# Turned tiles by transposing transfers of 1 MB for two tiles instead of 512 KB for one, with other buffer rings and a new order of the work

## The chip, the core and the metric

The kernel runs on one core of one Trainium2 chip. The metric is the time of one execution in device microseconds (us); lower is better. Data lie in HBM, in on-chip memory of 128 partitions, and in PSUM, the accumulators that the matrix engine writes. The engines have separate instruction queues and wait for one another by semaphores: PE (matrix multiply), DVE (vector), ACT (scalar functions), POOL (a second elementwise engine) and SP (which here only issues transfers).

## What is computed

An attention through 49 agent rows per batch, then a feed-forward layer with a softmax gate (SoLU) and a normalisation over the 1024 hidden values. There are 4 batches of 12608 tokens with 128 channels. Cut to what matters:

```python
def _attn_ref(q, k, v, agents):
    ...
    a2k = sm(agents, k)          # 49 x 12608 per batch
    agent_v = a2k @ v            # 49 x 128
    q2a = sm(q, agents)          # 12608 x 49
    return q2a @ agent_v

def _moe_ref(x, w_in, w_out, g_ln):
    h = x @ w_in                                  # 50432 x 1024
    e = np.exp(h - h.max(-1, keepdims=True))
    sm = e / (e.sum(-1, keepdims=True) + 1e-09)
    solu = h * sm
    mu = solu.mean(-1, keepdims=True)
    var = ((solu - mu) ** 2).mean(-1, keepdims=True)
    ln = (solu - mu) / np.sqrt(var + 1e-06) * g_ln
    return ln @ w_out                             # 50432 x 128
```

## The kernel before

Tokens are handled in 394 tiles of 128. A batch first runs **phase A** (L600 to L753): its keys and values come in 13 chunks, scores, exponentials and the sums over tokens give a small matrix, which is multiplied with w_in. The first batch's phase A opens the program; those of the other three run between the tiles of the batch before. **Phase B** (L862 to L909) makes, for eight tiles at a time, the softmax of the queries against the agents, as the stationary operand `pT`.

Each tile x then goes through this chain, and its names are those of the profile:

- **H** (L954, PE): four 128x512 products into `ph`, one of two PSUM buffers of 1024 columns.
- **max** (L985, DVE): copies `ph` to `e` and takes the row maximum; **exp** (L992, ACT) writes over `ph`; **U** (L1000, DVE) multiplies the two into `u`, one of six buffers. The next H on this `ph` waits for U.
- **square** (L1020, ACT): the sum of squares of `u`.
- **turning**: the second product needs `u` with the 1024 hidden values on the partitions. 63 of the 394 tiles (two in 13, and the last two) are turned on PE (L1026) and copied out of PSUM by ACT or DVE (L1031) into a `t` buffer. The other 331 are split into two 16-bit halves, F0 (L1008 on POOL, or L1006 on ACT) and F1 (L1011, POOL), in an `f` buffer, and SP issues a transposing transfer from `f` to an `x` buffer (L1015).
- **W** (L1047, PE): 24 16-bit products of 128x128 for such a tile (8 of 32 bits for one turned on PE), added up in a PSUM bank `px` that holds four tiles.
- **output**: DVE (L1100) or ACT (L1098) scales four tiles into `ob`, and SP stores eight tiles at a time (L1106).

There are five `f` buffers of 512 KB, eight `x` and eight `t` buffers of 512 KB. The `x` and `t` buffers also take the first batch's keys and values (L583, L589). SP issues everything that moves, in one order: transposing transfers, keys (L583), values (L589), queries (L841) and stores (L1106). An instruction that waits on SP holds all that stands behind it.

The order of all engines is a table. `plan.op` (L175) declares each piece of work with its engine, its cost and what it depends on; `Plan.run` (L188) walks the compressed list `STEPS` and emits the pieces in that order, and a bit beside each entry picks the engine where two are allowed. The costs decide only how many filler products PE runs in waits at the start (L1116), and which PSUM bank a piece takes. For a transposing transfer the four numbers in L1195 are what the planner assumes of it: how long SP is held (`XHOLD`), the shortest distance between two landings, the time from the hold's end to the landing (`XLAG`), and its kind.

```python
F1[x] = op("G", F(c_f1, x), 2.098, at(x, DF1, DUR, DUL), [F0[x]])
XT[x] = op("S", F(c_x, x), (XHOLD, 1.95, XLAG, 1), at(x, DX, DUR, DUL),
           [F1[x], W[fl[-1 - XB]] if len(fl) > XB else mdone[0][0]],
           after=[XT[fl[-2]] if len(fl) > 1 else None])
```

Of the kernel before, what the change touches and what calls it, by code (L numbers as in the profile page):

```python
# [13 lines left out]
F32 = mybir.dt.float32  # L14
# [3 lines left out]
F16 = mybir.dt.float16  # L18
# [11 lines left out]
    "VtHE%Qy5VvJ%YylIydemA0P_$CR8toyFdhy*0z&Jm*HgWZ9zPg(0=Itu^ZoT@{io;7N9r@!EC6}2?EYX|&FGz!sWSVQzTOMq{{3$imTjre6!Krc_zS;G"  # L30
    "YCWz30GOqY$N808r>Qy5%NLYj_Ew;)sIP3U;U?ajoAKTOsC&_$I+<B0U!*}DJbC%)YY*OE#hY+zHn|=qP8|((b1?TDFSH#?uA&XqRdoLYdjDy2@5mP9b"
    "wXW5*byc(DMJ7oLr2513)=f{E`9PdfBuuoaI3O0+__y=5d7L#DwH6=qmD=Ywx3f~w=3(s=Zq?}d>%fajxDABI=CvDZ&%LMLDAN}J+wg{f<K*vWq_NDb8"
    "bR|*>WMkdhoHQ3@*}PV8n$BlCx{`L7lG$b)@Cq#B5QQ$LCRIn$<c`dxzBLL|JG&bdGNUKKo)Ns{n4@EmD5zckDD5b{f;+2|PH+bWOu<P`MA){V@CB6b<"
    "m0R1_bEs%QGiaBq45;7`=g6BWSz(hIw^$o?z8=0^YgtG~QcK!YUtPk*5i+B~?DsR?dsc&Yfm_KTyPB`z`}AGSZDZ40N+I*YfKphcPrwn)wEgml4hD-60"
    "J4Lv>-O#HEt02EOB^m9Vi0a`{}wRKAuIezczqeZv{F9*DpH25Ty7P)Ic_MEK1D^Lge@!dB2nyYC2bANpMrLqoWeHVJ4b@uVCF7-A7>Fr8`&BH*E{i#|#"
    "qd=7kO3``|JbP6%hznP<T`<yu55K&<4MC7=YFwl+J7*2D;KSdB!jYC2pf=GI7)on~z;g0*Q7i7DduWwFB~jf!^^Ji1ypWKb(&x~gaR!il9pK;pARN#ve"
    "60C*{}Yd%PJ2l09_c3CJ?GcYuQxu;2tDd3Ssh!KJ?o8R>?ssJ1HM>rd8bPrwmMQat1HTB_FBa{UVWsZk?&2;6p=jlp0e!(P*#-Mu_jm`uoK)Fd)l`QDX"
    "#vE46=Hd+y+B!F69gVGyP=`QHhJ%$6T4;`F7USy8oQod%;IqR5&<EmhOw`-Vd}8b<E}Mn9ANeDn5hSLDKRZ>bZ~HbP$x*?r9&!Rwjh#^|fiTPSi@3<Tv"
    "gvA7P}CUeZz+fSKx#{s3&}FE3R;^tQNQ-Yw4;4uj%_#%C@F&sQ|m?cReF>V#=8Tz6hL_n#l6+$tE!fQkVSrg1`NCUq6bGCtGxB<Lqoz5n6ITjV<v;3{*"
    "-^EEvUo$U{NjkI=1fliD)`jk4uV84|*1*=NFGk@L%4giuu9WDL!ffir2+S(CLFT5EjlnI%kc4!<q=qvCXc(PP{Fm<Bk9KQSszNyJtVe*BEhR{TX!hgWC"  # L40
    "N55?AJ%j73)p+X_>8NuN4+adZ<(A9`x`=1EHSgYZb3V;IMVt3@H;uuo+GPx<z9;ZwKhxc+EVQH9r_(C}q5F_uG732}*-v1r9csc3NP)?R4dl_D+BnyYP"
    "vw?6T##`HGT6tx^jx;@Dhlm<H1L3svX6dKh9CXg_n&<H&oaFG*?;rToqVOMRrqVAdY_h%;f-+clM(w!huz%-qi4`Ejt@M#QR-5r)S9U={~~1n(YF<sf2"
    "izE;>XcdFLy~ZzU?}`Q$*AXxX~D>y0_AG@9Dx$?%@6H(n-Jju&w(ps4edC!K3oh9Ui)AaGJWD`zjv_oo<zQe>Fl#fn#_&_c-U2+Mjp#$cO~{^;`LvK%V"
    "pKB7T={x|XSTRNhpinq34I1T1*05LF`n>1N`q00@raS2Bw61n>}M2qBK+4-T3Z2H-wC9NVWaOGlKoJ{d;9yLh&^6r!L0?@k^_RkQoWDbGo!YoFRP@$C>"
    "Pho6rWW(_al6g7&!1OHTZy6iAg^s!H`6$5Mo$=tg+K|D1LxITcFWB5dE)sfFn)GF`Lfrsq5-(RFlDoJ(w*INAUjmgEzIgu4<Fpl|sS}`@;4#!HH-|ebR"
    "JArfPy_iTLq$1cULqI;wp*tO9Xy+zf&I#<_-stWrc$ISuuv@+Df{T1wx-wflQ+=o$m(nApt!u6UmQLx~oghwdkeLrNAx|Eh-J(nQy?*=@it=*0iePt(A"
# [24 lines left out]
    "t7~MeQgxp;!s3&ffAhtrfB4gnMn3i-dm&_r84Bu3eV*Wfr}^*ywdXK7;XO}k_D=0eZ^yGrve9z)xQPrNKXP+Ncdw8UC+rmuq4rRwz0((|*IRmKP^&L?k"
    "J8QYlO9d1JhgWY=R<JAzBe`IUCB9t>dnFp7$WL4X;41%J1tZGKvBhU8mzmI&uD56J>jmvt-twF<8jEtp>EmBFH!qC*jKy-n|a$V1<Ok^)0BCT|LAZaJV"
    "8i)!Y5FSk2b@qypWn+LG2qV@f|#c{%`%}N)}e+xUt6%!xhgu^B?@iuVRTcRSRkKv@+nhN$>1JH8?fvc07IvP^32P2NnM}Keccd%kJS($Xv{I6bwF^T=)"
    "2%KFD{7C-<SLrIOCq9LQKppCYn0j8%fa5IV7#ZJnyA+wdT!d))HG#siv5PkA78H2$xzD2+1hee9aJBYZiX8a$|+tIWOC?e{hNDhc%$t$RhfG*-e$_xg*"
    "vvaS5=ne7|5mo`^#Osb#yrXph~j8trRpXa`SBS%+N#sB$RDC+VCN^pWxps9O%9z+!^hYP03c^bG1)#>8xJYFYDYZWJHCn;xXT=Fk?+c4;!9+I_;kNt#C"
    "B~XDmIf6Nq(G1g`hK;guWLi-i<bCIpL!NvTVd{K^<A6IJ)zIiZreniD{Q++V>RC*@_kBxCo{HSNUA;xzl1)?laDBfhgnHeb<vJWi9-X|WG<imSO&ox>c"
    "vi?Ofstx(2Y6OH*HqFq?QxUdX;M(Ul6Qn99*>-iR8Zxke44i`3z<E!kulLKZ{M76<CElN6wtgScy`M{W*YEg%@ovi`Cs(szQC*kPrrY7vb(D+&(0x&I="
    "WhWp7!)C=543FYz-c}>Zu>nHb#02pTqm~>z7ECYNg-Za~%sY_ekpBeAw5hjCh~xId_ugx&`-d6|Zfi-B8xBwqE<lKPf+6uLIbS$@9a#8x=%6n*a532C4"
    "W)I#tu}wQoHf6(&q2xJfkAx@R+W*4OO?#jUm-_}05&xH=8(j#3W_8=qlmdHsA;{p25yW@8}?oXlNruC1#p=GO{5WpISG@3_x{h3;_cl!xS!?s35&u0hi"
    "6AwxX`*KlJ8e<q1qf~y#6JIvUo$NmEZXf(q5PVQ=2E{H~ghZIyiKfm4t%f8Hm`><$d3Eq8rdtfOvhgj|G><eKyBPyaU1$hrfhy3@tAdl|ksSh8w<@-EE"  # L80
# [152 lines left out]
def kernel(  # L233
# [35 lines left out]
    XLAG = 2.45  # L269
# [1037 lines left out]
```

## Time and profile before

| | us |
|---|---|
| median of 3 runs | 1245.5 (1243.91 to 1249.04) |
| the profiled execution's own time | 1243.39 |
| its span, first to last instruction | 1241.6 |
| PE busy | 1205.5 (97%) |
| DVE busy | 1189.2 (96%) |
| ACT busy | 1179.8 (95%) |
| POOL busy | 1131.3 (91%) |

The profiled execution lies 0.5 below the lowest of the three runs and 2.1 below their median. Some 1.8 of its time lie around the span. The granted TensorE clock is 0.997 of full over the span, so PE runs at its upper level, 2.4 GHz. The ends of PE's products are modelled and overlap, so its 97% is not 97% of what it could do.

### The profile page before, as it was taken

What the parts mean: (1) busy time and instruction counts of PE and PEld (TensorE: products, weight loads), DVE (VectorE), ACT (ScalarE), POOL (GpSimd) and SP (SyncE); (2) the same over time, 40 slices, a digit from 0 to 9 for tenths busy, and PEclk for the clock granted to TensorE, in tenths of its full rate; (3) what the DMA queues carried; (4) which work ended last, traced back from release to release, by engine and by line L of the source; (5) the groups of instructions that cost most, each with busy time, mean ns of one, the idle gap of its engine ahead of it and who ended that gap; (6) DMA issues with size and microseconds to landing.
All of it is one profiled execution on the core that took longest, in us unless ns stands there. A gap on an engine that the chain in (4) does not pass through costs nothing.

```text
span 1241.6 us, 36546 instructions
## 1 busy us (share of the span) xinstructions
PE 1205.5 (97%) x14305; PEld 933.0 (75%) x14305; DVE 1189.2 (96%) x2207; ACT 1179.8 (95%) x2304; POOL 1131.3 (91%) x989
## 2 busy tenths in 40 slices
PE   7989999999999999999999999999999999999998
PEld 4667777777777877777777777777887777777777
DVE  6799999999999999999999999999999999999997
ACT  5599999999999999999999999999999999999997
POOL 3489999999999999898999999989999999999995
PEclk9999999999999999999999999999999999999999
DMA  9599999999999999999999999999999899898997
GB/s 366 209 209 235 244 254 233 236 243 190 222 227 225 248 216 239 266 275 222 232 205 192 244 240 253 245 254 235 235 220 201 188 203 221 181 201 192 198 193 174
DMA packets 721518, 281.43 MB, mean 227 GB/s; under 512 B 692672, under 2 KB 696256, under 8 KB 721344
## 3 DMA queue, kind: packets, MB, share of 16 engines
q1 hardware_dynamic: 721344, 279.08, 104.6%
q8 instruction: 112, 1.84, 0.6%
q14 instruction: 62, 0.51, 0.1%
HBM read 79.67 MB, written 25.82 MB: 85 GB/s over the span
## 4 chain that ended last, share of the span: by engine, by line
PE 29%; ACT 26%; DVE 14%; issue 13%; POOL 11%; DMA 6%; SPq 0%; DVEq 0%; POOLq 0%; ACTq 0%
PE px L1047 13%; ACT ph L992 11%; PE ph L954 8%; ACT sq_b L1020 5%; ACT sq_a L1020 4%; DVE e_b L985 3%; PE px L653 2%; DVE e_a L985 2%; PE px L600 2%; POOL f_b L1011 2%; PE px L1026 1%; POOL f_c L1011 1%; DVE u_e L1000 1%; POOL f_d L1011 1%; DVE u_a L1000 1%
## 5 line engine op out<-in xcount | busy, mean ns | idle before, releaser
L992 ACT ACTIVATE ph<-e_a,nm 128x1024 f32<-128x1024 f32 x197 | 219.0, 1112 | 8.7 <-DVE e_a L985 7.9
L992 ACT ACTIVATE ph<-e_b,nm 128x1024 f32<-128x1024 f32 x197 | 219.4, 1113 | 7.6 <-DVE e_b L985 6.3
L1000 DVE SCALAR_TENSOR_TENSOR u_d<-e_b,cb,ph 128x1024 f32<-128x1024 f32 x66 | 84.1, 1274 | 2.3 <-ACT ph L992 1.7
L1000 DVE SCALAR_TENSOR_TENSOR u_f<-e_b,cb,ph 128x1024 f32<-128x1024 f32 x65 | 82.8, 1273 | 2.8 <-ACT ph L992 2.2
L1000 DVE SCALAR_TENSOR_TENSOR u_a<-e_a,cb,ph 128x1024 f32<-128x1024 f32 x66 | 84.1, 1274 | 1.0 <-ACT ph L992 0.3
L1000 DVE SCALAR_TENSOR_TENSOR u_e<-e_a,cb,ph 128x1024 f32<-128x1024 f32 x65 | 82.9, 1275 | 2.1 <-ACT ph L992 1.4
L1000 DVE SCALAR_TENSOR_TENSOR u_c<-e_a,cb,ph 128x1024 f32<-128x1024 f32 x65 | 82.8, 1274 | 1.8 <-ACT ph L992 0.9
L1000 DVE SCALAR_TENSOR_TENSOR u_b<-e_b,cb,ph 128x1024 f32<-128x1024 f32 x65 | 82.8, 1274 | 1.8 <-ACT ph L992 1.4
L1047 PEld LDWEIGHTS <-x_c 128*128 128x128 f16 x1008 | 61.9, 98 | 13.5 <-issue 3.6
L1047 PE MATMUL px<-wh,x_c 128*128 128x128 f16 x672 | 70.3, 219 | 1.0 <-DMA x_c<-f_e 0.7
L1020 ACT ACTIVATE sq_a<-u_c 128x1024 bf16<-128x1024 f32 x66 | 69.5, 1053 | 1.8 <-DVE u_c L1000 1.4
L1020 ACT ACTIVATE sq_b<-u_d 128x1024 bf16<-128x1024 f32 x66 | 69.3, 1051 | 1.9 <-DVE u_d L1000 1.5
L1047 PEld LDWEIGHTS <-x_b 128*128 128x128 f16 x1008 | 61.0, 98 | 13.3 <-issue 3.1
L1047 PE MATMUL px<-wh,x_b 128*128 128x128 f16 x672 | 68.9, 219 | 1.8 <-DMA x_b<-f_b 1.3
L1047 PE MATMUL px<-wh,x_f 128*128 128x128 f16 x656 | 68.0, 219 | 2.3 <-DMA x_f<-f_d 1.2
L1020 ACT ACTIVATE sq_a<-u_a 128x1024 bf16<-128x1024 f32 x66 | 69.4, 1052 | 0.8 <-DVE u_a L1000 0.4
L1020 ACT ACTIVATE sq_b<-u_b 128x1024 bf16<-128x1024 f32 x66 | 69.4, 1052 | 0.3
L1047 PE MATMUL px<-wh,x_e 128*128 128x128 f16 x656 | 69.1, 219 | 0.3 <-DVE ob_b L1100 0.2
L1047 PE MATMUL px<-wh,x_h 128*128 128x128 f16 x656 | 68.9, 219 | 0.5 <-DMA x_h<-f_a 0.5
L1047 PEld LDWEIGHTS <-x_e 128*128 128x128 f16 x984 | 60.1, 98 | 11.9 <-issue 2.2
L1047 PEld LDWEIGHTS <-x_a 128*128 128x128 f16 x1008 | 61.0, 98 | 10.4 <-issue 2.3
L1020 ACT ACTIVATE sq_a<-u_e 128x1024 bf16<-128x1024 f32 x65 | 68.3, 1051 | 0.5
(450 smaller groups left out, 5069.7 us busy)
## 6 DMA issues: line engine op xcount, KB each, us to landing
qt_a<-in_qT_dram SPq DMA_DIRECT2D x24, 512.0 KB, 5.1
qt_b<-in_qT_dram SPq DMA_DIRECT2D x24, 512.0 KB, 5.2
out_dram<-ob_a SPq DMA_DIRECT2D x24, 512.0 KB, 4.0
out_dram<-ob_b SPq DMA_DIRECT2D x24, 512.0 KB, 4.5
vt_b<-in_v_dram SPq DMA_DIRECT2D x18, 512.0 KB, 5.2
kt_a<-in_kT_dram SPq DMA_DIRECT2D x18, 512.0 KB, 5.6
kt_b<-in_kT_dram SPq DMA_DIRECT2D x18, 512.0 KB, 5.2
vt_a<-in_v_dram SPq DMA_DIRECT2D x18, 512.0 KB, 5.7
```

The lines of the kernel that those rows point to most:

```text
L600: nc.tensor.matmul(px[h * AP2 : (h + 1) * AP2, :w], ag_sb[:, b, :], kt[:, o : o + w], start=True, stop=True)
L653: nc.tensor.matmul(px[h * AP2 : (h + 1) * AP2, :C], eT[:w, o + h * AP2 : o + (h + 1) * AP2], vt[:w, t, :], start=all(z[0] != h for z in mm ...
L954: nc.tensor.matmul(ph[:, sl], w, m[:, sl], start=(q == 0), stop=(q == len(mm) - 1))
L985: nc.vector.tensor_scalar(out=nhs[x], in0=phs[x], scalar1=nks[k][:, j : j + 1], scalar2=None, op0=ALU.mult, op1=ALU.min, accum_out=nms[x])
L992: nc.scalar.activation(out=phs[x], in_=nhs[x], func=AF.Exp, scale=-1.0, bias=nms[x], accum_out=rs_[R]["S"][:, j : j + 1])
L1000: nc.vector.scalar_tensor_tensor(out=u, in0=nhs[x], scalar=scal(x)[:, 4:5], in1=phs[x], op0=ALU.mult, op1=ALU.mult, accum_out=rs_[R]["U"][ ...
L1011: nc.gpsimd.tensor_tensor(out=fs[x][:, 1, :], in0=us[x], in1=fs[x][:, 0, :], op=ALU.subtract)
L1020: nc.scalar.activation(out=sq, in_=us[x], func=AF.Square, scale=RN, accum_out=rs_[R]["Q"][:, j : j + 1])
L1026: nc.tensor.transpose(pt[:, kf * P : (kf + 1) * P], us[x][:, k0 * P : (k0 + 1) * P], ident)
L1047: nc.tensor.matmul(po, ut, wt[:, kf, :], start=(q == 0), stop=(q == len(mm) - 1))
```

## The change

- One transposing transfer turns two tiles, 1 MB. An `f` buffer is double and holds two tiles; there are three of them (six tiles instead of five). The transfer waits for the F1 of both tiles, and the first of the two tiles waits for the same transfer as the second. F0 of a pair's first tile waits for the transfer three pairs back.
- The turned tiles go to seven double buffers instead of eight single ones: the four double `x` buffers, and three of the four double `t` buffers read as 16-bit. Tiles turned on PE have two `t` buffers instead of eight.
- Of 331 transposing transfers 165 pairs and one single remain.
- The room for the sixth `f` tile comes from two small tiles of the start, `mean_sb` and `ws`, which now lie in the `ob` buffers.
- The planner's numbers for a transposing transfer become a hold of 2.4, a distance of 3.6 and a lag of 2.95 for a pair. `STEPS` is another list.

```diff
-    XB = 8
-    TBUF = 8
+    XP = 7
+    TBUF = 2
+    HB = 8
...
-    FBUF = 5
-    XHOLD = 1.6
-    XLAG = 2.45
+    FP = 3
+    XHOLD = 2.4
+    XLAG = 2.95
...
-    fr_, xr, tr = ring(FBUF, [P, 2, DF], F16, "f"), ring(XB, [P, 2 * NF, P], F16, "x"), ring(TBUF, [P, NF, P], F32, "t")
+    fpr, xpr, tpr = ring(FP, [P, 4, DF], F16, "f"), ring(HB // 2, [P, 4 * NF, P], F16, "x"), ring(HB // 2, [P, 2 * NF, P], F32, "t")
+    fr_, xr, tr = ([t[:, m * i : m * (i + 1), :] for t in z for i in range(2)] for z, m in ((fpr, 2), (xpr, 2 * NF), (tpr, NF)))
+    xps = xpr + [t.bitcast(F16).rearrange("p k (z t) -> p (k z) t", z=2) for t in tpr[TBUF // 2 :]]
...
-        mean_sb = bpool.tile([P, C], F32, tag="mean", bufs=1, name="mean_sb")
+        mean_sb = obr[0][:, 0, :]
...
     def c_x(x):
-        pr[x] = xr[fl.index(x) % XB]
-        nc.sync.dma_start_transpose(out=pr[x], in_=fs.pop(x).rearrange("p a f -> p (a f)"))
+        q = fl.index(x) // 2
+        m = min(2, len(fl) - 2 * q)
+        for i in range(m):
+            pr[fl[2 * q + i]] = xps[q % XP][:, 2 * NF * i : 2 * NF * (i + 1), :]
+        nc.sync.dma_start_transpose(out=xps[q % XP][:, : 2 * NF * m, :], in_=fpr[q % FP][:, : 2 * m, :].rearrange("p a f -> p (a f)"))
...
             F1[x] = op("G", F(c_f1, x), 2.098, at(x, DF1, DUR, DUL), [F0[x]])
-            XT[x] = op("S", F(c_x, x), (XHOLD, 1.95, XLAG, 1), at(x, DX, DUR, DUL),
-                       [F1[x], W[fl[-1 - XB]] if len(fl) > XB else mdone[0][0]],
-                       after=[XT[fl[-2]] if len(fl) > 1 else None])
-            need, step, c = [[XT[x]], [XT[x]]], 6, 0.0557
+            if i % 2 == 0:
+                XT[q] = op("S", F(c_x, x), (XHOLD, 3.6, XLAG, 1), at(x, DX, DUR, DUL),
+                           [F1[x], W[fl[2 * (q - XP) + 1]] if q >= XP else mdone[0][0]], after=[XT.get(q - 1)])
+            else:
+                XT[q].deps.append(F1[x])
+                XT[q].left += 1
+                F1[x].outs.append(XT[q])
+            need, step, c = [[XT[q]], [XT[q]]], 6, 0.0557
```

What the new list does to the order is seen at two places. The names are those of the chain above; `kt`, `vt` and `qt` are keys, values and queries.

SP, about tile 217, in phase A of the third batch, before: four plain loads stand together ahead of a transposing transfer.

```order
L1015 DMA_TRANSPOSE x_g<-f_c 128x16x128
L583 DMA kt_a<-in_kT_dram 128x1024
L841 DMA qt_b<-in_qT_dram 128x1024
L583 DMA kt_b<-in_kT_dram 128x1024
L841 DMA qt_a<-in_qT_dram 128x1024
L1015 DMA_TRANSPOSE x_h<-f_d 128x16x128
L1015 DMA_TRANSPOSE x_a<-f_e 128x16x128
L1015 DMA_TRANSPOSE x_b<-f_a 128x16x128
L1015 DMA_TRANSPOSE x_c<-f_b 128x16x128
```

SP, the same tiles after the change (the pair that holds tile 217 is `x_a<-f_b`):

```order
L1021 DMA_TRANSPOSE t_c<-f_c 128x32x128
L1112 DMA out_dram<-ob_b 128x1024
L844 DMA qt_b<-in_qT_dram 128x1024
L586 DMA kt_a<-in_kT_dram 128x1024
L1021 DMA_TRANSPOSE t_d<-f_a 128x32x128
L1021 DMA_TRANSPOSE x_a<-f_b 128x32x128
L592 DMA vt_b<-in_v_dram 128x1024
L592 DMA vt_a<-in_v_dram 128x1024
L586 DMA kt_b<-in_kT_dram 128x1024
L1021 DMA_TRANSPOSE x_b<-f_c 128x32x128
```

The transfers are half as many and twice as large, go to `x` and `t` buffers in turn, and plain transfers stand between them more often: in the whole order 177 plain transfers between transposing ones stood in 68 groups, and 176 now stand in 87.

POOL, some way before that, before the change: F0 and F1 of three tiles, each into an `f` buffer of its own, with the normalisation's small steps between.

```order
L1008 TENSOR_SCALAR f_e<-u_c 128x1024
L1011 TENSOR_TENSOR f_d<-u_b,f_d 128x1024
L1011 TENSOR_TENSOR f_e<-u_c,f_e 128x1024
L1008 TENSOR_SCALAR f_a<-u_e 128x1024
L1067 TENSOR_TENSOR U_7990<-U_7990 128x16
L1068 TENSOR_TENSOR Q_7989<-Q_7989,U_7990 128x16
```

POOL, the same place after the change:

```order
L1011 TENSOR_SCALAR f_b<-u_b 128x1024
L1014 TENSOR_TENSOR f_b<-u_b,f_b 128x1024
L1011 TENSOR_SCALAR f_c<-u_c 128x1024
L1014 TENSOR_TENSOR f_c<-u_c,f_c 128x1024
L1011 TENSOR_SCALAR f_c<-u_e 128x1024
L1073 TENSOR_TENSOR U_7902<-U_7902 128x16
```

The instructions are the same; two tiles (`u_c` and `u_e`) now write one buffer `f_c`, and the transfer of it stands behind the later F1.

## Rows read from the trace of the kernel before

**Rows 1.** The page, busy us of each engine, share, and instructions.
```profile
PE 1205.5 (97%) x14305; PEld 933.0 (75%) x14305; DVE 1189.2 (96%) x2207; ACT 1179.8 (95%) x2304; POOL 1131.3 (91%) x989
```

**Rows 2.** Windows of start, middle, end: us, PE, PEld, DVE, ACT, POOL busy, clock, DMA.
```profile
0.00:124.00 124.00, 110.36 (x1151) 74.17 (x1152) 104.35 (x227) 95.43 (x198) 82.19 (x86) 0.97 0.90 255
124.00:1178.00 1054.00, 1036.34 (x12466) 809.22 (x12466) 1031.15 (x1888) 1028.51 (x1999) 999.45 (x847) 1.00 1.09 226
1178.00:1242.00 64.00, 58.80 (x693) 49.66 (x690) 53.71 (x94) 55.86 (x109) 49.69 (x58) 0.99 0.83 182
```

**Rows 3.** Windows of 62 us: one inside phase A, one behind the last.
```profile
744.00:806.00 62.00, 60.16 (x732) 47.09 (x729) 59.08 (x104) 58.91 (x110) 59.02 (x50) 1.00 1.16 246
1054.00:1116.00 62.00, 59.22 (x712) 47.18 (x712) 61.66 (x110) 61.66 (x113) 60.50 (x56) 1.00 0.95 194
```

**Rows 4.** Line 1015: who waited (us, times), and issue to landing.
```profile
  PEld L1047: 11.5, 15
  PE px L1047: 4.8, 6
...
DMA to landing us min/median/max: 3.6/4.7/11.5
```

**Rows 5.** Line 985: DVE idle before it until (us, times).
```profile
  PE ph L954: 8.1, 22
```

**Rows 6.** Timelines of DVE, POOL and PE: start us, us, tile 217's U, F1, W.
```profile
718.27 1.27 DVE L1000 SCALAR_TENSOR_TENSOR u_b<-e_b,cb,ph 128x1024 f32<-128x1024 f32 x1
...
725.46 2.14 POOL L1011 TENSOR_TENSOR f_d<-u_b,f_d 128x1024 f16<-128x1024 f32 x1
...
738.97 0.22 PE L1047 MATMUL px<-wh,x_h 128*128 128x128 f16 x1
```

**Rows 7.** Timeline of SP about the same tile.
```profile
725.04 0.52 SPq L583 DMA_DIRECT2D kt_a<-in_kT_dram  x1
...
726.55 0.43 SPq L841 DMA_DIRECT2D qt_a<-in_qT_dram  x1
727.62 7.72 SPq L1015 DMA_TRANSPOSE x_h<-f_d  x1
735.44 1.70 SPq L1015 DMA_TRANSPOSE x_a<-f_e  x1
```

**Rows 8.** DMA issues from 724 to 745, last column us from issue to landing.
```profile
qt_a<-in_qT_dram SPq DMA_DIRECT2D x1, 512.0 KB, 8.9
...
x_h<-f_d SPq DMA_TRANSPOSE x1, 9.6
```

**Rows 9.** Timeline of SP, two transposing transfers back to back.
```profile
136.09 1.82 SPq L1015 DMA_TRANSPOSE x_c<-f_d  x1
138.01 1.83 SPq L1015 DMA_TRANSPOSE x_d<-f_e  x1
```

**Rows 10.** DMA issues from 125 to 141, the same two.
```profile
x_c<-f_d SPq DMA_TRANSPOSE x1, 4.0
x_d<-f_e SPq DMA_TRANSPOSE x1, 3.9
```

**Rows 11.** Single lines of DVE, ACT and POOL: ns min/median/max.
```profile
L1100 DVE TENSOR_TENSOR ob_a<-px,yc x41: 674/684/690, 91.2 to 1234.1; 128x512 f32<-128x512 f32 x41
...
L612 DVE TENSOR_SCALAR nmp<-mxp,nmp x34: 199/209/215, 13.6 to 882.9; 128x1 f32<-128x1 f32 x34
...
L892 POOL TENSOR_SCALAR pack<-logits x23: 295/530/557, 67.7 to 898.5; 128x392 f16<-128x392 f32 x21, 128x98 f16<-128x98 f32 x1, 128x147 f16<-128x147 f32 x1
...
L890 ACT CAST pack<-logits x29: 278/526/537, 20.1 to 1185.6; 128x392 f16<-128x392 f32 x27, 128x98 f16<-128x98 f32 x1, 128x147 f16<-128x147 f32 x1
```

**Rows 12.** Timeline of ACT: four tiles of output, and the next instruction.
```profile
143.90 1.12 ACT L1098 ACTIVATE ob_a<-px,yc 128x128 f32<-128x128 f32 x4
144.90 1.06 ACT L1020 ACTIVATE sq_a<-u_c 128x1024 bf16<-128x1024 f32 x1
```

**Rows 13.** Timeline of PE's weight loads: the 24 of one tile's W.
```profile
605.03 1.44 PEld L1047 LDWEIGHTS <-x_b 128*128 128x128 f16 x24
```

More of the change, by code (lines that the diff above doesn't have):

```diff
@@ L30 @@
[L30 to L34, printed above, removed]
@@ new lines @@
+    "o^T^wbwcG`6~rk)fQvO{k~u7|4jJE@)hhAB`^^Dn+AH*BOefLuf2P#%flo&s&{ow3(pq*6COzrcoGg463hKbXY_+U2S~>R<B=mt*N*UN!+qx%P}st3W<"
+    "~aF&zkf$6JMkC`QFeczu5}wv(do;At5p!W%TM^~J>&m>MOl>-Fhnb!;sWCrRS9q_)V@cfnqEVx<=rG`5$bS35fK_|g+A-ELxqvL5jD`57bEf8L1|7aIs"
+    "M%?3_ayT<kTv@(>&`!BYaLtoaf;$rQ?y(9{03}VEj>CZl~io*^~rp00r7n9ZRa$?2BRna;{9^bg6dI_jGvC=glw3>m&_(9hsq?E?>qvKAjqP?29dYHyF"
+    "2wr+(rE4qbg}ByPG_EP2bFQv+5_by1#da>@PgOJ=5Z7>{aX$OMJh9RcvBqjIIkD1fg81@*zU;&*J~g$XPj@Qu^G~eweXe&AgdF{UIkBSupH8fFaQ`kRR"
+    "{tAJ&l;5"
@@ L456, in sums @@
             if q == 0:
-                pm["s"] = epool.tile([P, NF // 2, C], F32, tag="sq", bufs=1, name="ws")
+                pm["s"] = obr[1][:, : NF // 2, :]
             a = w2 if q == 0 else pm["s"]
@@ L581, in kload @@
             w = CT * P if c < NCK else CKT
-            kts[c] = xr[c % XB].rearrange("p a t -> p (a t)").bitcast(F32) if head else ktr[(c + b) % 2]
+            kts[c] = xr[c % HB].rearrange("p a t -> p (a t)").bitcast(F32) if head else ktr[(c + b) % 2]
             nc.sync.dma_start(out=kts[c][:, :w], in_=kT[b, :, c * CT * P : c * CT * P + w])
         def vload(c):
-            vt = tr[c % TBUF] if head else vtr[(c + b) % 2].rearrange("p (j d) -> p j d", d=C)
+            vt = tr[c % HB] if head else vtr[(c + b) % 2].rearrange("p (j d) -> p j d", d=C)
             vts[c] = vt
@@ L769, in kop @@
             if c < NC and c not in K:
-                old = M1.get(c - 2) if not head else M1.get(c - XB)
+                old = M1.get(c - 2) if not head else M1.get(c - HB)
                 K[c] = op("S", st(kload, c), sz(c), -199 + 0.2 * c if head else at(c * 2.55 - 3), gate + [old])
         def vop(c):
-            old = M2.get(c - 2) if not head else M2.get(c - TBUF)
+            old = M2.get(c - 2) if not head else M2.get(c - HB)
             V[c] = op("S", st(vload, c), szv(c), -199 + 0.2 * c + VLAG if head else at(c * 2.55 - 2), gate + [old])
@@ L1003, in c_f0 @@
     def c_f0(x, k="G"):
-        f = fs[x] = fr_[fl.index(x) % FBUF]
+        f = fs[x] = fr_[fl.index(x) % (2 * FP)]
         if k == "A":
@@ L1188 @@
         if xbar(x):
+            i = len(fl)
+            q = i // 2
             fl.append(x)
-            old = XT[fl[-1 - FBUF]] if len(fl) > FBUF else None
-            F0[x] = op("GA" if FLEX or len(fl) % 3 == 0 else "G", F(c_f0, x), (1.02, 0.937) if FLEX or len(fl) % 3 == 0 else 1.05, at(x, DF0, DUR, DUL),
-                       [U[x], old] + ([] if old else wready if len(fl) % FBUF == 0 else cin if len(fl) < 3 else cout),
-                       after=[F0[fl[-2]] if len(fl) > 1 else None])
+            old = XT.get(q - FP)
+            F0[x] = op("GA", F(c_f0, x), (1.02, 0.937), at(x, DF0, DUR, DUL),
+                       [U[x], old] + ([] if old or i > 4 else wready if i == 4 else cin if i < 2 else cout),
+                       after=[F0[fl[-2]] if i else None])
             F1[x] = op("G", F(c_f1, x), 2.098, at(x, DF1, DUR, DUL), [F0[x]])
-            XT[x] = op("S", F(c_x, x), (XHOLD, 1.95, XLAG, 1), at(x, DX, DUR, DUL),
-                       [F1[x], W[fl[-1 - XB]] if len(fl) > XB else mdone[0][0]],
-                       after=[XT[fl[-2]] if len(fl) > 1 else None])
-            need, step, c = [[XT[x]], [XT[x]]], 6, 0.0557
+            if i % 2 == 0:
[6 more added lines that the diff above has]
+            need, step, c = [[XT[q]], [XT[q]]], 6, 0.0557
         else:
```

214 lines of the change are left out of this document (107 added, 107 removed).

## The prediction

> **What bounds the kernel now.** I read the page's busy times first [rows 1]: four engines lie between 91% and 97%, so none has room for the work of another, and the question is what idle time is left. The table of windows splits it [rows 2]. DVE is idle for 124.00 - 104.35 = 19.7 us at the start, 1054.00 - 1031.15 = 22.9 in the middle and 10.3 at the end. In the middle ACT has 25.5 and POOL 54.6. DVE is the fullest engine of those whose busy time is not modelled, and its middle is the place to look at. A window behind the last phase A shows how full it can be, 61.66 of 62; one inside a phase A has 59.08, with more DMA traffic (1.16 against 0.95) [rows 3]. At the rate of the better window the 1054 us of the middle, 17 windows, would hold 17 x 0.34 = 5.8 us of idle DVE, so **17.1 us is the most that any better order can win there** with the same work.
>
> Next I ask what DVE waits for. In front of its maximum it was idle for 8.1 us, in 22 cases, because PE's H came late [rows 5]. And PE was late partly because of the turned tiles: W waited for a transposing transfer 15 times, 11.5 us in all on the weight loads (the 4.8 on the products are part of the same waits) [rows 4]. That is few of 331 transfers. Tile 217 shows why they are late at all: its F1 ends at 727.60, SP issues the transfer at once, but behind four plain loads, and SP is held 7.72 us [rows 6, 7]. It lands 9.6 us after the issue, at 737.2; the median is 4.7 [rows 4, 8]. W follows at 738.97, 1.75 later [rows 6]. Back to back without such a burst two transfers land 4.0 and 3.9 us after issues that are 1.92 apart [rows 9, 10], so one flows in 138.01 + 3.9 - 136.09 - 4.0 = 1.8 us.
>
> **The change, part by part.** The page holds no transfer of 1 MB, so its price is bounded. If the number of transfers decided, a pair would flow in 1.8 and land after 3.9, as one does now; if two go one behind the other and nothing overlaps, it would land after 7.8. I take two that flow in a row, since the rows are two such transfers and bytes double: flow 3.6 to 3.8, landing 1.8 + 3.9 = 5.7. The two ends stay for the range.
>
> The Trainium skill, page "DMA: Bandwidth & Descriptors", section "Latency and other measured facts", gives transposing transfers 261 GB/s when the middle dimension isn't contiguous. An estimate from that is 4.0 us of flow for 1.05 MB. The trace's 1.8 us for 0.52 MB is 290 GB/s, near enough that by either the bytes decide and a pair saves no flow. By the skill's rate taken alone, with nothing else gained, the sum would be that of the first rival below, 1245; by the rows it is the forecast.
>
> Transfers on SP: 165 issues fewer. Each holds SP about 1.8 us when the queue is full [rows 9], and the hold is the flow itself, so I count nothing for it; what hides it is that SP issues ahead of W. What is gained is room for the plain loads: before, 68 groups stood between the transfers, now 87, so a transfer meets shorter bursts. Each change of kind could cost from 0 to about 1.4 us of queue time (the last load of tile 217's burst lands at 726.55 + 8.9 = 735.45, its transfer 1.8 later, so no cost is seen there). 19 more would be 0 to 27 us of queue time. It is hidden as long as the queue is not the bound, and it costs in the phase A windows if it is.
>
> The first tile of a pair waits for the second's F1 and for the longer transfer. Counted in PE's order between tiles 20 and 370, the number of H issued when W starts, less the tile's index, was 8.0; counted from the pair's later tile it is now 7.5 for a pair's first W and 8.6 for its second. A tile takes 1241.6 / 394 = 3.15 us of the span, so the first W has 0.53 x 3.15 = 1.7 us less room, and its transfer lands 5.7 - 3.9 = 1.8 later. **It loses 3.5 us of slack**, where tile 217 had 1.75. The second loses nothing: +1.9 of room, -1.8. So the gain must come from the bursts being shorter: tile 217's transfer took 5.7 more than an undisturbed one. If loads are spread so that half of this goes, the first tiles stand about where they stood. I take the net on PE's waits as a gain, because the seven double buffers also let a transfer go 14 tiles ahead instead of eight, and because the order was made with a landing of 0.09 + 2.4 + 2.95 = 5.4 for a pair, 0.3 below my 5.7, as it was made before with 4.1, 0.6 below the median 4.7: the pairs' assumption is no further off than the old one. The gain: **-7 us**, most of the 8.1 that DVE lost to late H [rows 5], between -17.1 (the most above) and +14 (the rival below).
>
> The moved work, from counts of the two orders: 10 outputs of four tiles go from DVE to ACT. On DVE two such follow each other at just under their 684 ns, so -6.8; on ACT four pieces take 144.90 - 143.90 = 1.0 [rows 11, 12], so +10.0. Back come 5 copies of turned tiles and 3 of phase A from ACT to DVE, priced on both like the 128x512 output, 0.68 (+5.4 on DVE, as much off ACT); 7 small minima from POOL to DVE at 0.21, +1.5; 7 casts of `pack` from ACT to POOL at 0.53, -3.7 on ACT and +3.7 on POOL [rows 11]. DVE: +0.1; ACT: +0.9; POOL: at most +3.7. The last two are covered by their 25.5 and 54.6 of idle time [rows 2]; without that cover they would cost as much as they are. PE does the same products. So no engine is relieved: **0 us** (-1 to +2).
>
> The end: after the last H, PE has the 24 products of one more tile to do, 605.03 to 606.47 or 1.4 us [rows 13]: **+1.4**, less if PE would have waited there (0 to +1.4). The start: the first transfer waits for a second F1, but nothing on DVE, ACT or POOL waits for the first W; **0** (0 to +2, if PSUM banks run out). The small tiles that went to `ob` are used before the first output: 0.
>
> Sum, on the profiled execution's 1243.4: -7 + 0 + 1.4 = 1237.8. That execution lies 2.1 below the runs' median, so the forecast for a run is **1238**, at the favourable end of 1237.8 to 1239.9.
>
> **The rivals.** *Bytes decide and nothing is won.* The waits on transfers fall in the phase A windows and rise elsewhere, because every first tile has less slack; DVE's 22.9 stays. For it: the flow of a pair is that of two, the engines' work is the same. Against it: 11.5 us of waiting are there to be removed. Time 1243.4 + 1.4 = 1245. The Trainium skill's 261 GB/s, named above, speaks for this one.
>
> *Slower: the first tile of each pair comes late.* Place: W of a pair's first tile on PE, then the H behind it, then DVE. 166 transfers late by 0.1 us more on the mean are 16.6 us on PE; DVE lost 8.1 where PE lost 11.5, so 0.70 of it, 11.7 us. Time 1243.4 + 11.7 + 1.4 = 1256.5. It decides when landing passes 5.7 plus what the shorter bursts give back, say 8: then a first tile with the slack of tile 217 is late by 4. For it: 3.5 us is twice tile 217's slack. Against: only 15 of 331 waited before, so the usual slack is larger.
>
> *A larger gain*: landing well under 5.7, DVE as full as behind the last phase A: 1243.4 - 17.1 = 1226.
>
> That the change isn't made as described is excluded by the order: 165 transfers of 128x32x128 and one of 128x16x128.
>
> **How the numbers follow.** A measurement of this kernel tells about 0.5% from no change, 6.2 us. The forecast and the larger gain together have 0.46, nothing won 0.28, slower 0.26. The range goes from 1226 to 1257: below lies about 0.06, above about 0.12. The forecast's own range is 1231 to 1241.
>
> **What would show it.** Right: waits of W for transposing transfers under 11.5 us, DVE's idle in the middle near 15, landing of a pair near 5.7 where no load stands ahead. Nothing won: landing as said, but DVE idle near 23. Slower: the waits of W several times 11.5, all on a pair's first tile. I am wrong altogether if POOL waits for its `f` buffers or the start grows by more than 2 us.

## The result and the profile after

| | before | after |
|---|---|---|
| median of the comparison's four runs each, us | 1247.3 (1243.9 to 1249.0) | 1262.4 (1260.4 to 1268.9) |
| profiled execution's own time | 1243.4 | 1260.4 |
| its span | 1241.6 | 1258.6 |
| transposing transfer, us to landing, min/median/max | 3.6/4.7/11.5 | 3.9/7.1/12.1 |

The changed kernel is slower: ratio 1.0134, 95% interval 1.0089 to 1.0179. The forecast was 1238, and the range ended at 1257, 5 below the median.

The page's busy times, against [rows 1]:

```profile
PE 1208.2 (96%) x14305; PEld 934.1 (74%) x14305; DVE 1188.9 (94%) x2214; ACT 1182.8 (94%) x2329; POOL 1132.6 (90%) x989
```

No engine got more work to speak of: DVE -0.3, ACT +3.0, POOL +1.3. The 17.0 us of span are idle time. The windows of [rows 2], now with the end at 1258.6 (columns as there: stretch, length, then PE, PEld, DVE, ACT, POOL):

```profile
0.00:124.00 124.00, 107.65 (x1107) 70.79 (x1108) 101.78 (x221) 93.45 (x194) 79.43 (x85) 0.99 0.84 249
124.00:1178.00 1054.00, 1028.08 (x12392) 804.42 (x12390) 1021.32 (x1878) 1020.99 (x2005) 991.19 (x839) 1.00 0.99 224
1178.00:1259.00 81.00, 72.46 (x813) 58.91 (x810) 65.83 (x117) 68.39 (x132) 61.97 (x67) 0.98 0.80 172
```

DVE is idle for 22.2 us at the start (19.7 before), 32.7 in the middle (22.9) and 15.2 at the end (10.3): +2.6, +9.8 and +4.9.

Who waits for a transposing transfer, line 1021 now, against [rows 4]:

```profile
  PEld L1053: 33.8, 32
  PE px L1053: 25.0, 25
  POOL f_b L1011: 3.0, 2
...
DMA to landing us min/median/max: 3.9/7.1/12.1
```

W's weight loads wait 33.8 us in place of 11.5. DVE's maximum hands it on; its idle time until H, line 988 now, was 8.1 in [rows 5]:

```profile
  PE ph L957: 21.5, 36
```

**One such wait, followed through the engines.** POOL's timeline first (start us, us, engine, line, what): the F1 of the two tiles of a pair in buffer `f_a`.

```profile
329.10 2.13 POOL L1014 TENSOR_TENSOR f_a<-u_b,f_a 128x1024 f16<-128x1024 f32 x1
...
332.35 2.13 POOL L1014 TENSOR_TENSOR f_a<-u_d,f_a 128x1024 f16<-128x1024 f32 x1
```

SP's timeline: a store, then the pair's transfer, issued 0.03 us behind the second F1, 3.28 behind the first.

```profile
332.10 0.52 SPq L1112 DMA_DIRECT2D out_dram<-ob_a  x1
334.51 3.90 SPq L1021 DMA_TRANSPOSE x_b<-f_a  x1
```

Its landing, from the DMA issues of 331 to 337 (last column: us from the issue):

```profile
x_b<-f_a SPq DMA_TRANSPOSE x1, 7.3
```

So it lands at 341.8. PE's timeline: the last product of the tile before, the first of this pair's first tile, and the H behind it.

```profile
340.10 0.22 PE L1053 MATMUL px<-wh,x_a 128*128 128x128 f16 x1
341.90 0.23 PE L1053 MATMUL px<-wh,x_b 128*128 128x128 f16 x1 [1.58 <-DMA x_b<-f_a]
...
342.91 0.38 PE L957 MATMUL ph<-mh,pT_d 128*128 128x512 f16 x1
```

DVE's timeline: the maximum that needs this H.

```profile
343.98 1.28 DVE L988 TENSOR_SCALAR_CACHE_REDUCE e_b<-ph,nk_d 128x1024 f32<-128x1024 f32 x1 [0.67 <-PE ph L957]
```

PE loses 1.58, DVE 0.67 of it. All 25 waits of products in the trace are of this kind: on the first product of a pair's *first* tile. None is on a second tile, which is turned by the same transfer but used one tile later.

The 3.9 in the row of landings is the one single transfer; a pair's shortest is 5.5 us, with little beside it. SP's timeline and the DMA issues from 626 to 636:

```profile
626.69 4.04 SPq L1021 DMA_TRANSPOSE t_d<-f_b  x1
634.66 4.01 SPq L1021 DMA_TRANSPOSE x_a<-f_c  x1
```

```profile
t_d<-f_b SPq DMA_TRANSPOSE x1, 5.5
x_a<-f_c SPq DMA_TRANSPOSE x1, 5.5
```

### The profile page after: what moved, and what is told of

Same layout as the page of the kernel before. It is cut to its first block, busy times and chain, and to the rows that moved or that the text cites. A ratio compares the mean times of both kernels' runs of the same rounds, so it can differ in the third digit from the quotient of the medians.

```text
span 1258.6 us, 36086 instructions
## 1 busy us (share of the span) xinstructions
PE 1208.2 (96%) x14305; PEld 934.1 (74%) x14305; DVE 1188.9 (94%) x2214; ACT 1182.8 (94%) x2329; POOL 1132.6 (90%) x989
## 4 chain that ended last, share of the span: by engine, by line
PE 26%; DMA 18%; DVE 16%; POOL 15%; ACT 14%; issue 10%; SPq 0%; POOLq 0%; DVEq 0%; ACTq 0%
PE px L1053 12%; PE ph L957 7%; ACT ph L995 6%; POOL f_a L1014 4%; DVE e_b L988 4%; DVE e_a L988 3%; ACT sq_b L1026 3%; POOL f_b L1014 3%; DMA x_a<-f_a 3%; POOL f_c L1014 2%; ACT sq_a L1026 2%; PE px L656 2%; DMA x_b<-f_a 2%; DMA t_b<-f_b 2%; POOL f_b L1011 2%
## 5 line engine op out<-in xcount | busy, mean ns | idle before, releaser
L1053 PE MATMUL px<-w,t_a 128*128 128x128 f32 x1008 | 137.9, 279 | 0.5 <-DVE ob_b L1106 0.5
L1053 PEld LDWEIGHTS px<-w,t_a 128*128 128x128 f32 x1008 | 127.3, 192 | 11.1 <-issue 2.8
L1053 PE MATMUL px<-wh,x_a 128*128 128x128 f16 x768 | 79.4, 220 | 6.3 <-DMA x_a<-f_a 5.5
L1053 PE MATMUL px<-wh,x_c 128*128 128x128 f16 x768 | 79.3, 220 | 5.1 <-DMA x_c<-f_a 2.2
L1053 PEld LDWEIGHTS <-x_d 128*128 128x128 f16 x1152 | 68.9, 98 | 12.1 <-issue 2.4
L1053 PE MATMUL px<-wh,x_d 128*128 128x128 f16 x768 | 76.3, 220 | 1.4 <-DMA x_d<-f_a 1.4
L1053 PE MATMUL px<-wh,t_b 128*128 128x128 f16 x752 | 75.4, 220 | 2.0 <-DMA t_b<-f_a 1.5
L1053 PE MATMUL px<-wh,t_d 128*128 128x128 f16 x736 | 73.6, 220 | 3.5 <-DMA t_d<-f_b 2.0
L1053 PEld LDWEIGHTS <-t_b 128*128 128x128 f16 x1128 | 67.5, 98 | 12.6 <-issue 2.6
L1053 PEld LDWEIGHTS <-t_d 128*128 128x128 f16 x1104 | 66.3, 98 | 14.1 <-DMA t_d<-f_b 2.5
```

What stands on the lines that cost most here:

```text
L1053: nc.tensor.matmul(po, ut, wt[:, kf, :], start=(q == 0), stop=(q == len(mm) - 1))
```

## The experiments

All ratios are to the kernel before, run beside them on the same chip. "W's waits" are those of its weight loads for transposing transfers (before: 11.5 us; after: 33.8).

### Size, order or buffers

Three theories stood at first: A, a pair's first tile comes late by the long transfer; B, the new list of steps is worse whatever the transfers; C, the buffers.

**The old list on the new buffers**, one transfer per tile into half of a double buffer (no other edit):

> The kernel before with its old list and single transfers, but with the new buffers (six f tiles, 14 turned tiles, two t buffers, the two small tiles of the start in ob). Theories A and B: as before, within 0.5% (1241 to 1253). Theory C: 1256 or more.

1248.8, ratio 1.0010 (0.9994 to 1.0026); W's waits 14.8. The buffers are not the cause.

**The old list with pairs**: where both tiles of a pair are ready before the first's W in the list, one transfer of 1 MB at the second tile's place (129 pairs), the rest single.

```diff
+        if i == 0 and paired.get(q):
+            return
+        two = i == 1 and paired.get(q)
+        a, b = (0 if two else i), i + 1
+        nc.sync.dma_start_transpose(out=xps[q % XP][:, 2 * NF * a : 2 * NF * b, :],
+                                    in_=fpr[q % FP][:, 2 * a : 2 * b, :].rearrange("p a f -> p (a f)"))
```

> The kernel before with its old list, but with the new buffers and with 1 MB transfers at the place of the second tile's transfer wherever the old list has that ahead of the first tile's W (129 pairs; 73 tiles keep single transfers). Theory A: the old list has even less room for a pair, W's waits for transfers grow above 60 us, and the time is 1265 to 1300. Theory B: the pairs do little harm, 1245 to 1255. Theory C: as slow as the changed kernel, about 1262.

1346.1, ratio 1.0794 (1.0761 to 1.0827), above theory A's range. Then **two transfers of 512 KB at that same place**:

```diff
-        a, b = (0 if two else i), i + 1
-        nc.sync.dma_start_transpose(out=xps[q % XP][:, 2 * NF * a : 2 * NF * b, :],
...
+        for a in range(0 if two else i, i + 1):
+            nc.sync.dma_start_transpose(out=xps[q % XP][:, 2 * NF * a : 2 * NF * (a + 1), :],
...
```

> The old order with the new buffers; where the run with the old order issued one transfer of 1 MB for two tiles (129 times), this one issues two of 512 KB, one behind the other, at that same place. Theory S (the size costs: one long hold): 1265 to 1300, well under the 1346 of the transfers of 1 MB. Theory P (the place costs: the first tile of a pair is issued at the second's place, by whatever transfer): 1325 to 1350.

1256.7, ratio 1.0085 (1.0056 to 1.0114), under theory S's range. Who waited, first with pairs, then with two transfers at the pair's place:

```profile
  PEld L1066: 101.4, 55
  PE px L1066: 84.5, 48
...
DMA to landing us min/median/max: 3.7/5.8/11.9
```

```profile
  PEld L1066: 18.5, 14
  PE px L1066: 13.7, 10
...
DMA to landing us min/median/max: 3.6/4.6/11.1
```

The late place on SP costs 0.85% at most, one transfer in place of two the other 89 us. Not all of the 89 is waiting: with pairs the granted clock was 0.976 and PE busy 1234.0 us, with two transfers 0.995 and 1211.1. The first of two needs only its own F1 and lands by itself; the pair waits for the second F1 and lands later. Theory A has its mechanism, in the old list.

**The new list with each pair split into two transfers**, at the pair's place:

```diff
-        nc.sync.dma_start_transpose(out=xps[q % XP][:, : 2 * NF * m, :], ...
+        for i in range(m):
+            half(q, i)
```

> The changed kernel, but each pair's 1 MB transfer is issued as two of 512 KB at the same place in the order, both behind the second F1; buffers and order unchanged. Theory A (the size of the transfer and the pairing make a pair's first tile late): the first half lands about 1.8 us earlier than the pair did, so of the 33.8 us of W's waits for transfers about half goes and the time falls to 1248 to 1256. Theory B (the new list is the loss, made with a hold of SP of 2.4 where the chip shows 4.0): SP is held as long as before, the time stays at 1257 to 1264. Theory C (the buffers): stays at 1260 to 1264.

1263.2 (1255.6 to 1269.0), ratio 1.0133 (1.0082 to 1.0183), in the ranges of B and C, where A had wanted 1248 to 1256. **The first half at its own place** on SP, as far as the list's reckoning tells it:

> The new order with two transfers of 512 KB per pair, the first put on SP ahead of the first load, store or transfer that the list's own reckoning starts behind that tile's F1; where nothing stands between, the two are adjacent, as in the run with the split. The pairing is undone as far as the list allows. Theory R: the first tile's turning lands some 2 us earlier where a load stood between, so less than the 1263 of the split: 1246 to 1256. Theory Q: SP's holds are the same in sum, and loads behind two transfers are late: 1258 to 1266.

1269.5, ratio 1.0169 (1.0127 to 1.0212), above both theories' ranges. W's waits fell to 23.0 and 18.0, and the time did not:

```profile
  PEld L1058: 23.0, 21
```

```profile
  PEld L1072: 18.0, 15
```

SP's timeline of the first of these runs (its trace is that of the longest run, 1269.0) shows another cost (x2: both halves of a pair and what lies between them):

```profile
620.16 4.03 SPq L1017 DMA_TRANSPOSE t_b<-f_c  x2
624.28 5.87 SPq L1017 DMA_TRANSPOSE t_c<-f_a  x2
630.25 4.17 SPq L1017 DMA_TRANSPOSE t_d<-f_b  x2
634.52 5.34 SPq L1017 DMA_TRANSPOSE x_a<-f_c  x2
```

The first half goes behind its own F1, and SP stands in the two for 4.0 to 5.9 us here; in the last row 1.6 of it is the wait for the second F1. Over the whole trace the median is 5.5 a pair, where the changed kernel's one transfer holds SP 4.2, and the holds add up to 913 us in place of 778. What stands behind is issued later. The longest waits of PE for values and keys in the `vt` and `kt` buffers (us, times, longest), of which the changed kernel has 0.5 us in all:

```profile
PE px L656 <- DMA vt_a<-in_v_dram: 2.9, 1, 2.9
PE px L603 <- DMA kt_a<-in_kT_dram: 2.7, 1, 2.7
```

So one cost was taken away and another put in. That the two cancel is argued from these rows and not shown; by the times alone these runs speak against A. **The first half right behind its F1 in the order of emission** put it ahead of loads that were due before:

> The changed kernel, but the first tile of a pair gets a transfer of 512 KB of its own, issued right behind its own F1, and the second tile one at the pair's old place; buffers and the rest of the order unchanged. Theory A: nothing of the pairing is left, W's waits for transfers fall to 12 us or less, and the time comes to 1238 to 1250. Theory B: the list keeps most of the loss, 1255 to 1264. Theory C: 1260 to 1264.

1440.3, ratio 1.1562 (1.1523 to 1.1602), outside every theory's range: W's waits 103.8, and PE waits 12 to 18 us on each of four buffers that plain loads fill. It tells only that SP's order cannot be changed so.

### How long the transfer is

The cleanest question leaves list and places alone and changes the number of bytes. Half and three quarters of each pair from the eighth on (the rest of what W reads is old):

```diff
+        a, b = (1, 3) if q >= XP and m == 2 else (0, 2 * m)      # (1, 4) for three quarters
+        nc.sync.dma_start_transpose(out=xps[q % XP][:, NF * a : NF * b, :], in_=fpr[q % FP][:, a:b, :]...
```

> The changed kernel with every full transfer from the eighth on moving two of its four quarters (0.52 MB: one half of either tile); the other half of what W reads is old, so half of the turning is left out. Hold and flow of such a transfer are those of a single one before, about 1.9 us in place of 4.1, where the list was laid out with a hold of 2.4 and a flow of 3.6. Theory L (the new list is good, but a transfer of 1 MB holds SP and the queue longer than the list was laid out for): 1230 to 1248, waits of W for transfers under 15 us, the waits of DVE's maximum for H back at 8 or less. Theory N (the new list itself couples the engines worse, whatever a transfer costs): 1256 to 1264.

> The same with three of four quarters (0.79 MB), a quarter of the turning left out: hold about 3.0, flow about 2.9, landing about 4.7. Theory L: between the half and the whole, 1242 to 1254, nearer to the half if the hold of 2.4 is the point from which it costs. Theory N: 1256 to 1264.

1238.1, ratio 0.9937 (0.9913 to 0.9961), and 1239.1, 0.9943 (0.9925 to 0.9961). The half lies inside theory L's range and three quarters 3 us under it; N falls. The half has one more difference: it needs no second F1 (it moves the first tile's low and the second's high part), so three quarters is the run to go by. Its transfers (line, tile, count, hold in ns min/median/max), who waited, and landings:

```profile
L1022 SPq DMA_TRANSPOSE x_a<-f_c x8: 2980/3058/3926, 174.4 to 1197.8; - x8
...
  PEld L1054: 7.2, 8
  PE px L1054: 4.5, 5
...
DMA to landing us min/median/max: 4.2/5.4/9.8
```

and the middle window:

```profile
124.00:1178.00 1054.00, 1042.54 (x12576) 817.55 (x12573) 1035.83 (x1908) 1035.34 (x2038) 1008.41 (x855) 1.00 0.81 190
```

One quarter less in a transfer, 1.0 us of hold and 1.7 us of median landing, is worth 1.0134 - 0.9943 = 1.9%, 24 us. DVE's idle time in the middle is 18.2, where the forecast said "near 15". The same with half of each tile's transfer **in the kernel before**:

```diff
+        a = 1 if fl.index(x) >= XB else 0
+        nc.sync.dma_start_transpose(out=pr[x][:, NF * a :, :], in_=fs.pop(x)[:, a:, :]...
```

> The kernel before with every transfer from the ninth on moving one of its two halves (0.26 MB): half of the turning is left out. What the waits on transfers were worth in the old order. If they were worth what the forecast took (7 us): 1238 to 1242. If W's late starts were hidden or came from the list and not from the transfers: 1244 to 1247. Both theories leave this open; it sizes the gain that was there to be had.

1238.5, ratio 0.9937 (0.9916 to 0.9958), inside the range for waits worth what the forecast took:

```profile
  PEld L1048: 1.7, 2
  PE px L1048: 0.7, 1
...
DMA to landing us min/median/max: 2.7/2.8/9.4
```

So up to 7.8 us were to be had from the transfers in the old list (the run halves their bytes and holds too, not the waits alone). With half the bytes old and new list come to the same ratio, 0.9937: with W's waits nearly gone, the new list shows neither a gain nor a loss against the old.

### Is it the wait, or the hold

A longer transfer makes W wait, and it also holds SP and the queue. Theory R says the first, Q the second. Six runs gave W more room in PE's order, the first three by one H: the first tiles' W, both tiles' W, and all W in the old list with single transfers.

```diff
+            if xbar(x) and (len(fl) - 1) % 2 == 0:    # first tiles; all tiles in the next
+                plan.later.add(o)
...
+        for i, k in self.moved(todo):                 # held until one more H has been emitted
```

> The changed kernel; on PE the products W of each pair's first tile stand one tile's H later in the order than the list puts them (what depends on them follows; the second tile's W is pushed by 0.4 of an H with it). The transfers, their size and their place on SP stay. Theory R (a pair's first W has too little room between landing and its place): 0.6 of an H more, about 1.8 us of room, takes two thirds of the waits away, as the transfer of three quarters did with 1.3 more: 1240 to 1252, waits of W for transfers under 20 us on the weight loads. Theory Q (SP and the queue are too full with 4 us of hold, and what is late there would be late anyway): 1257 to 1265.

> The same for both tiles of each pair: every W of a tile turned by a transfer stands one H later. Theory R: as the run before, 1239 to 1251; the second tiles did not wait and give nothing more. Theory Q: 1257 to 1265.

> The old order with one transfer per tile and the new buffers (1248.8 before this edit), every W of a tile turned by a transfer one H later: the seven double buffers have the place for it. Theory R: the waits of W on transfers (14.8 us on the weight loads) mostly go, 1239 to 1245, under both kernels. Theory Q: 1246 to 1252.

1537.0 (ratio 1.2332, 1.2297 to 1.2367), 1653.7 (1.3277, 1.3223 to 1.3331) and 1657.4 (1.3305, 1.3253 to 1.3358). The edit was bad: pieces of W that stood between the halves of H came out in one bunch in front of an H. DVE's largest wait in the first of them (us, times, longest):

```profile
DVE e_b L1016 <- PE ph L985: 136.9, 81, 5.0
```

These say nothing on R or Q, but how tight PE's order is. **Shifted within W's own places**, by a tile, by half a tile, and by half a tile in the old list with single transfers:

```diff
+        ws = [z for z in todo if z[0] in self.later]
+        due = [(ws[slot[i] - 4] if slot[i] >= 4 else None) if i in slot else (i, k) for i, k in todo]   # 2 for half a tile
```

> The changed kernel; the places in PE's order at which the list puts pieces of W stay, and what stands in them is shifted by four pieces, one tile: every W comes one tile later (a first tile's W 9.5 H behind in place of 8.7), in bursts no longer than before, which the two runs with W behind the next H had not kept (their pieces came out bunched in front of an H). Transfers stay as they are. Theory R (a pair's first W has too little room): 3 us more room takes nearly all waits on transfers away, 1238 to 1248. Theory Q (4 us of hold fill SP and the queue, and what they make late is late anyway): 1257 to 1266.

> The same shifted by two pieces, half a tile, some 1.3 to 1.6 us of room: as much as the transfer of three quarters gave, with all four quarters moved. Theory R: 1241 to 1252. Theory Q: 1257 to 1266.

> The old order, one transfer per tile, the new buffers (1248.8 without this edit), the contents of W's places shifted by two pieces. Theory R: the old order's waits on transfers go too, 1240 to 1246. Theory Q: 1246 to 1252.

1281.0 (1.0288, 1.0260 to 1.0316), 1263.6 (1.0149, 1.0126 to 1.0171) and 1255.8 (1.0079, 1.0053 to 1.0105): R's numbers missed three times. The second lies in Q's range, the other two above it. In the run shifted by a tile the waits are gone and others stand in their place:

```profile
  PEld L1073: 0.5, 1
...
DMA to landing us min/median/max: 4.6/7.0/11.7
```

```profile
PEld L977 <- issue: 56.6, 111, 2.8
...
DVE ob_a L1126 <- PE px L1073: 13.0, 7, 3.8
```

Outputs now wait for W (13.0 us on one buffer), and the weight loads of H stand idle for 56.6 us without a wait that the profile shows (32.8 in the changed kernel). In the old list, where there was less to win, half a tile cost 1255.8 against 1248.8. A list made tight elsewhere doesn't give W room for nothing, so these runs don't separate R from Q.

**The run that does** takes away only what makes the first tile wait: its W reads the second tile of the pair before, by other data. Transfers, places, products and order stay.

```diff
+        if q >= XP:
+            pr[fl[2 * q]] = xps[(q - 1) % XP][:, 2 * NF :, :]
```

> The changed kernel in which, from the eighth pair on, W of a pair's first tile reads the second tile of the pair before (landed long since) in place of its own turned tile: what makes it wait is gone, and the turning of the first tiles is left out of the result. Every transfer of 1 MB, its place on SP, its hold, its flow, every product and every place in PE's order stay; the second tile's W still waits for its own transfer. Theory R (the loss is the first tile's W): 1236 to 1246, waits of W for transfers under 15 us. Theory Q (4 us of hold on SP and the queue make other work late): 1254 to 1264.

1243.4, ratio 0.9972 (0.9958 to 0.9986). Who waited, and the middle window:

```profile
  PEld L1055: 3.6, 4
...
  PE px L1055: 1.6, 2
...
DMA to landing us min/median/max: 3.9/7.1/12.0
```

```profile
124.00:1178.00 1054.00, 1040.84 (x12544) 815.85 (x12542) 1034.51 (x1905) 1033.18 (x2035) 1005.78 (x849) 1.00 1.02 227
```

The landings are those of the changed kernel, 7.1, and 1.0134 - 0.9972 = 1.6%, 20 us, are gone. That is theory R's range, and 11 us under Q's. What is left for Q in the last quarter of a transfer is the 0.3% between this run and that with three quarters, and their intervals just overlap. The shift by half a tile, which gave Q's number, and the split, which missed A's, left the first tile's need in place and put other costs in; this run puts none in.

### A list for the true length

Can an order hide a transfer of 1 MB? The changed kernel's list was searched on by local moves, with prices near the profile's; so was the old list with single transfers on the new buffers.

```diff
-    XHOLD = 2.4        # 1.6 in the old list
-    XLAG = 2.95        # 2.45
+    XHOLD = 3.93       # 1.75
+    XLAG = 2.9         # 2.3
-        "SP": 0.0, ... "SG": 0.0
+        "SP": 1.0, ... "SG": 0.5       # 1.5 and 0.75
-            (XHOLD, 3.6, XLAG, 1)
+            (XHOLD, 4.0, XLAG, 1)
```

> The changed kernel, same code, same buffers, same transfers of 1 MB; only its list of steps is searched on by local moves (a step past its neighbours on its engine, or to the other engine that may take it) with prices for a pair's transfer near those that the profile showed: hold 3.93 in place of 2.4, flow 4.0 in place of 3.6, and turned tiles usable 7.9 us after the issue in place of 5.4 (profiled median 7.1). It changes the order all over, so it tells not which step counts but whether an order laid out for the transfer's true length exists. Theory R (the list left a pair's first tile too little room; the size as such can be hidden): waits of W for transfers under 10 us, 1230 to 1243. Theory Q (4 us of hold on SP and the queue cannot be hidden by any order): 1250 to 1262.

> The old code with the new buffers, one transfer of 512 KB per tile; its old list searched on in the same way with hold 1.75, flow 1.95 and turned tiles usable 5.6 us after the issue (profiled median 4.7; the old price was 4.1). Theory R: 1230 to 1241, as a transfer of half the size gave in the old list or less; within 4 us of the pairs with true prices, which would say that pairing as such neither costs nor gives. Theory Q: 1238 to 1246 here and some 10 to 20 us under the pairs.

1254.3, ratio 1.0053 (1.0034 to 1.0071), and 1250.7, 1.0037 (1.0020 to 1.0053). The pairs lie in Q's range, where R had wanted 1243 or less; the single transfers lie above both ranges. The two are 3.6 us apart, as R had it, where Q had 10 to 20. The pairs are 8 us better than the changed kernel, and W still waits:

```profile
  PEld L1080: 16.6, 13
  PE px L1080: 10.6, 10
...
DMA to landing us min/median/max: 4.4/7.3/12.9
```

The search had tiles usable 7.9 us after the issue, above the median and below the longest landings. It also moved small work: POOL waited 21.9 us for DVE's maxima of phase A, 2.3 before. So a list searched with a price nearer the truth takes part of the loss away, and these searches found none that beats the kernel before; whether one exists, and with it whether a transfer of 1 MB can be hidden, stays open. So does what decides how far a landing lies above its quiet value.

## Why the prediction was wrong, step by step

**What bounds it: right.** DVE's middle was the place, and turned tiles were what to win there. The 7 us of the forecast were there: up to 7.8 by the run of the kernel before with half transfers.

**The price of a transfer: right, but of a quiet one.** The landing of 5.7 came out as 5.5 where little stands beside it, and "flow 3.6 to 3.8" as a hold of 3.9 to 4.0. The Trainium skill, page "DMA: Bandwidth & Descriptors", section "Latency and other measured facts", gives transposing transfers 261 GB/s when the middle dimension isn't contiguous; 1.05 MB in the 4.0 us of hold is 262, so trace and rule agree. What the kernel meets is the median, 7.1.

**The step that failed** is the sentence "So the gain must come from the bursts being shorter", with the term of -7 that hangs on it. It let half of what a burst costs a transfer come back, so that "the first tiles stand about where they stood". They did not. Half of all landings lay between 3.9 and 5.6 us before and lie between 5.9 and 7.7 now: the spread did not shrink, and the whole went up by about 2. The bursts did get shorter: directly behind a plain load on SP the median landing went from 6.8 to 7.4 us, less than the 1.8 of the longer transfer. But 68 of 331 transfers stood behind one before (21%), and 87 of 166 do now (52%); of W's 33.8 us of waits 24.3 are on those 87. The prediction counted how long a burst is and not what share of the transfers meets one. Counted over the timelines, the room between landing and W fell from a median of 3.6 us for a single tile to 1.5 for a pair's first tile. The "3.5 us of slack" that a first tile loses was the right warning, and 2.1 of it were not given back. In place of the 7 us of gain the span grew by 17.0, and the run in which the first tiles read older data gives 20 back. The argument that the list was laid out with a landing "no further off than the old one" compared 5.4 with the estimate 5.7; against the median it was off by 1.7, the old one by 0.6.

**The slower rival** had mechanism, place and readings right: all waits of products on first tiles, W's waits at three times the old value. Its price, 0.1 us per pair, was 22.3 / 166 = 0.13 measured on the weight loads; DVE lost 13.4 of 22.3 at the maximum, 0.60 where 0.70 was taken. Its point, a landing of 8, was too high: 7.1 is enough, and 5.4 is not. Weighing it 0.26 because "only 15 of 331 waited before, so the usual slack is larger" left the usual slack uncounted: 3.6 us less 3.5 leaves nothing.

**SP's hold counted as nothing:** nearly right for the changed kernel, by the run with old data, which keeps every hold and loses nothing by it. The waits of POOL for its `f` buffers, a sign of being wrong, were 3.0 us (4.9 before).

**Moved work 0: right.** DVE -0.3 (+0.1 foretold), POOL +1.3 (at most 3.7); ACT's +3.0 was foretold as 0.9.

**Start and end:** the start lost 2.6 on DVE, just over the bound of 2, and so a sign of being wrong. Whether the list or the size of the transfers costs it is not shown: the runs with half, three quarters and old data differ from the changed kernel only from the eighth pair on, issued at 122 to 125 us, and are idle 21.5, 22.4 and 21.0 there. The end lost 4.9 in place of 1.4; three waits of products for a pair, 2.2 us at 1193, 0.8 at 1222 and 0.5 at 1233, stand in it.

## What to carry to other kernels

A merged transfer delayed its first user twice here: it starts when the last part is ready, and lands when all of it has. Price both with the median under load, not with the quiet value, and count the usual slack of the first user before setting them against each other; here they were about equal, and the merge lost. To tell "the wait" from "the load on the queue", let the waiting instruction read older data and leave every transfer where it is.

## What had not been expected

- SP's hold does not go with the bytes. Where nothing stood ahead, a transfer of 0.26 MB held SP 1.23 us, 0.52 MB 1.3 to 1.6 (1.8 back to back, [rows 9]), 0.79 MB 3.0, 1.05 MB 4.0: little more from the first to the second, about double from there to the third. The median landing went 2.8, 4.0 (4.7 in the kernel before), 5.4, 7.1. Rows of 0.26, 0.52 and 1.05 MB, in the kernel before with half transfers, the changed kernel with half, and the changed kernel:

```profile
L1016 SPq DMA_TRANSPOSE x_e<-f_e x9: 1232/1233/2094, 80.8 to 1203.8; - x9
```

```profile
L1022 SPq DMA_TRANSPOSE x_b<-f_a x8: 1317/1603/1635, 179.0 to 1200.4; - x8
```

```profile
L1021 SPq DMA_TRANSPOSE x_a<-f_c x8: 3817/4036/4786, 176.4 to 1220.1; - x8
```

- The edge is sharp: with the same list three quarters of a pair are 0.6% faster than before and four quarters 1.3% slower.
- W's products bunched in front of an H, with the same instructions on every engine, cost 23 to 33%. The granted clock was 0.944 to 0.961 in those traces (0.997 before), and PE was busy for 1271 to 1304 us (1205.5 before), so slower products are part of it.
